# A channel-attention and gated-unit kernel: first chunk's weights kept on chip, squares of the second batch moved late, v's sums by DMA, first loads cut smaller

## The chip, the cores and the metric

The kernel runs on one core of a Trainium2 chip. The metric is the device time of one execution in microseconds (us), the median of three runs.

## The reference

For each of 4 batches, q, k and v are 6080 x 256 (tokens x channels). The columns of q and k are normalised over the tokens, their 256 x 256 product (over the tokens) goes through a softmax, and v is multiplied by it. The result, 24320 tokens of 256, goes through a gated unit with 2048 hidden columns:

```python
qn = q / (norm(q, axis=1) + 1e-6); kn = k / (norm(k, axis=1) + 1e-6)
a = softmax(kn.transpose(0, 2, 1) @ qn / tau)      # 256 x 256 a batch
x = (v @ a).reshape(24320, 256)
h = x @ w_in                                       # 256 -> 2048
out = (h * sigmoid(1.702 * h)) @ w_out             # 2048 -> 256
```

w_in and w_out come as 64-bit floats; the kernel reads their 32-bit words and makes float32 of them on chip.

## The kernel before, in words

The attention is folded into the weights: a batch's 256 x 256 softmax is multiplied into w_in once (`weights`, matmuls on line 744), and the tokens of v go straight through that product. Every float32 operand of these products is split in a high and a low part (`cast` on ScalarE, line 304, then `low` on VectorE, line 333), and a product is three matmuls (`three`, line 875): high-high, high-low, low-high. All the products of the main part are therefore on line 875.

A batch's 6080 tokens are worked in 6 chunks of up to 1024 columns, and a chunk in 8 pairs, each a pair of 128-column blocks of w_in. So there are 4 x 6 x 8 = 192 pairs, numbered by `place`. A pair has a front (seven products of v's parts and the weights, into the PSUM banks X, Y and Z, then the gate) and a back (the gated values times w_out, into banks O2, O3, O4, O7 and K). Front and back use a two-by-two scheme with seven products in place of eight, for which sums of v's quarters are made: `values` makes four of them a chunk on VectorE (lines 835, 836, 840 and 844) and splits seven operands. The very first chunk has a back with eight plain products (`FIRST`), so that the sums of w_out's blocks are not needed yet.

The scores of a batch: q and k come in tiles of 128 tokens. For batches 0 and 1 (`direct`) the tiles are multiplied as float32 (line 552) while ScalarE squares them and VectorE adds the squares to `acc` (line 312 by the helper); a unit is two tiles, there are 25 of them, and 4 tiles are one load into one of four staging buffers (gr0, gj0, gr1, gj1). Batch 0 does this at the very start, batch 1 right behind it and during the first chunk. Batches 2 and 3 do theirs in between the pairs of the batches ahead (`scores_at`), split in high and low parts (line 558), with the squares added to `acc` by accumulating DMAs from GpSimd's queue (`add_dma`, line 327), as are K's partial sums (`ka`, `kb`, `kc`). After the scores come the norms, the softmax (`finish`, in three steps) and the eight `weights`.

The weights' words: `win_convert` loads the words of a group of two pairs, for each half of the input rows; seven VectorE instructions make float32 and its low part, the result goes through the buffer "hl" to DRAM (`win_d`), and `weights` loads it from there. `wout_convert` does the same for one pair of w_out, with the sums of its blocks, through "hl" to `wout_d`; `fetch_wo` loads from there. The first group and the first two of w_out are converted at the start, the others during the first chunk.

The order of all work is set by a planner (`Plan`). Each piece of work is a node with an engine, a guessed cost, its predecessors and a due time; buffers are slots that a new user can have when the users of the old one are done. A list placement, repeated backwards and forwards, gives each node a start, and the program is issued in that order, each engine working through its own queue in order. Loads and stores are issued on the SP queue (line 292), accumulating DMAs on GpSimd's. So every edit to nodes moves the whole order.

Of the kernel before, what the change touches and what calls it, by code (L numbers as in the profile page):

```python
# [11 lines left out]
F32 = mybir.dt.float32  # L12
# [8 lines left out]
P = 128  # L21
# [19 lines left out]
class Node:  # L41
    __slots__ = ("eng", "cost", "lag", "fn", "deps", "uses", "due", "idx", "start", "left", "ready", "outs")

    def __init__(self, eng, cost, fn, deps, uses, due, lag, idx):
        self.eng, self.cost, self.fn, self.due, self.lag, self.idx = eng, cost, fn, due, lag, idx
        self.deps = [d for d in deps if d is not None]
        self.uses = list(uses)
        self.start = None


class Plan:
# [27 lines left out]
    def graph(self):  # L79
# [111 lines left out]

VSUM = lambda b, c: False
QSUM = lambda b: b >= 2
HIACT = True
TURNED = True
TAILX = True
STQ = False
# [20 lines left out]
def channel_attention_then_glu(  # L218
# [61 lines left out]
    win_d = dr.tile([NPAIR, P, 2, NC2, 2 * P], F32, name="win_d")  # L280
    wout_d = dr.tile([NPAIR, P, 2, NA + 1, P], F32, name="wout_d")
    w_d = [dr.tile([NPAIR, P, 2, NA - 1, P], F32, name=f"w_d{i}") for i in range(B)]
# [53 lines left out]

    g.add("DVE", 150, lambda: nc.vector.memset(ones, 1.0), due=-9e9)
    g.add("DVE", 60, lambda: nc.vector.memset(half, 0.5), due=-8e9)
    const_i = g.add("POOL", 2000, lambda: make_identity(nc, ident), due=-9e9)

    def full_bank(slot, due):

        b = bank(slot, "x")

        def fn():
            for i in range(HW // P):
                nc.tensor.matmul(
                    b()[:, i * P : (i + 1) * P], lhsT=ones, rhs=ones, start=i == 0, stop=True, skip_group_check=True,
                )

        return g.add("PE", 880, fn, (), [b], due)

    def keep_warm(n, deps, due, slot):
# [5 lines left out]

        return g.add("PE", 220 * n, fn, deps, [b], due)  # L360

# [62 lines left out]

    win_ready = {}

    def win_convert(grp, c, due, slot, lows, after=()):
# [9 lines left out]
        st = [  # L437
            load(
                lambda a=a: win_d[2 * grp + a, :, :, c, :],
                lambda a=a: hl()[:, :, a * 2 * P : (a + 1) * 2 * P], 256, [l], [hl], due + 1,  # L440
            )
# [6 lines left out]

    def wout_convert(u, due, slot, lows, after=()):
        raw = sbuf(slot, [P, 2, C, 2], U32, "words")  # L450
# [6 lines left out]
        n = to_float32(first, lows, raw, rs, due, True, f)  # L457
        st = sbuf("hl", [P, 2, 8, P], F32R, "cs")
        n = sums(f, [n], [f], due + 0.7)
        h = cast(lambda: st()[:, 0], lambda: f(), 8 * P, [n], [f, st], due + 1)  # L460
        l = low(lambda: st()[:, 1], lambda: f(), lambda: st()[:, 0], 8 * P, [h], [f, st], due + 1.1)
        wout_ready[u] = load(lambda: wout_d[u], lambda: st(), 1024, [l], [st], due + 1.2)


    class Attention:
# [19 lines left out]
        def load_direct(self, t0, room, slot, due):  # L485
            nt = min(room, T - t0)
            t = sbuf(slot, [P, 2, RT, C], F32, "raw4")
            cuts = range(nt + 1) if t0 == 0 else (0, nt)
            ns = []
            for a, z in zip(cuts, cuts[1:]):  # L490
                for i in range(2):
# [3 lines left out]
                    ))  # L495
            for o in range(nt):
                self.raw[t0 + o] = (t, o, ns[2 * o : 2 * o + 2] if len(ns) > 2 else ns)
            if nt < room and TAIL:
# [6 lines left out]
        def unit(self, u, due, after=()):  # L505
# [37 lines left out]
            for j in range(nt):  # L543
# [24 lines left out]
                news.append(n)  # L568
            if u == 0:
                self.acc_n = [g.add(  # L570
# [21 lines left out]
            else:  # L592
# [7 lines left out]
                    )  # L600
                ]

        def finish(self, slot):
# [128 lines left out]
    def weights(at, u, due, after=(), slot="Z", kept=None):  # L732

        wi = sbuf("wi", [P, 2, NC2, 2 * P], F32R, "wi")
        r = load(lambda: wi(), lambda: win_d[u], 512, [*win_ready[u], *after], [wi], due - 10)
        pb = bank(slot, "w")

        def fn():
            for i in range(NC2):
                ci = slice(i * P, (i + 1) * P)  # L740
                n = 0
                for l, m in ((0, 0), (0, 1), (1, 0)):
                    for j in range(NC2):
                        nc.tensor.matmul(  # L744
                            pb()[:, i * 2 * P : (i + 1) * 2 * P], lhsT=at.aT()[:, l, j, ci], rhs=wi()[:, m, j, :],
                            start=i == 0 and n == 0, stop=True, skip_group_check=True,
                        )
                        n += 1

        n = g.add("PE", 1440, fn, [at.a_h, at.a_l, r], [at.aT, wi, pb], due)  # L750
        f = sbuf(f"ra{u % 2}", [P, 8, P], F32, "wf")
# [368 lines left out]
    def fetch_wo(ck, p, u, due, after=()):  # L1120
        is_s = ck.kinds[p][2]
        cut = slice(1, 1 + NI) if is_s else slice(0, 4)

        def make(i):
            w = sbuf(f"wo{i}", [P, 2, NI, P], F32R, "wo")
            n = load(
                lambda: w()[:, :, : cut.stop - cut.start], lambda: wout_d[u, :, :, cut, :], 640,
                [wout_ready[u], *after], [w], due,
            )
            return w, n  # L1130

        return wo_slots.get((u, is_s), make)

    held = [None, {}]

    def fetch_wb(ck, p, pairs_of, due, after=()):
# [9 lines left out]
        if u not in places:  # L1146
            i = len(places)
            n = load(
                lambda: w()[:, i], lambda: wout_d[u, :, :, 1 + NI :, :], 256, [wout_ready[u], *after], [w], due,
            )  # L1150
# [33 lines left out]
    for u in range(2):  # L1184
        wout_convert(u, -55 + 4 * u, f"gi{u}", "oc1")
    nxt = Attention(1)
# [5 lines left out]
    for u in range(nu):  # L1192
        nxt.unit(u, -40 + 4.5 * u)


# [16 lines left out]
    def softmax_at(b, i):  # L1212
# [6 lines left out]
        return fn  # L1219

    def weights_at(b, u):
# [13 lines left out]
    for b in range(B):  # L1235
        for s in range(total):
# [56 lines left out]
```

## Time and profile before

| | |
|---|---|
| runs | 2083.36, 2083.2, 2081.8 us; median 2083.2 |
| the profiled execution's own time | 2082.57 us |
| its span, from first to last instruction | 2080.8 us |
| granted TensorE clock over the span | 0.999 |
| TensorE, VectorE, ScalarE, GpSimd busy | 99%, 95%, 83%, 5% |
| DMA | 457.76 MB, mean 220 GB/s |

A row of a view names the line, the engine (PE is TensorE, DVE VectorE, ACT ScalarE, POOL GpSimd, SPq the SP queue), the operation, the tile written and the tiles read, then its numbers. Busy time is the union of the instructions' drawn lengths; the ends of matmuls are modelled, since they overlap in the engine's pipeline.

### The profile page before, as it was taken

How to read it: one execution, taken by the hardware profiler on the slowest of the kernel's cores; microseconds unless marked ns; L12 is line 12 of the kernel's file. 1: busy time of each engine (PE TensorE's matmuls, PEld its weight loads, DVE VectorE, ACT ScalarE, POOL GpSimd, SP SyncE). 2: the span in 40 equal slices, each digit the busy share in tenths (PEclk: the TensorE clock that was granted, in tenths of full speed). 3: DMA queues.
4: the chain of work that ended last, by engine and by line, in shares of the span. 5: the costliest groups of instructions: out<-in, count | busy, mean ns of one | idle time of the engine just before them, and what ended most of it. 6: DMA issues, size and time to landing. Idle time of an engine off the chain costs nothing.

```text
span 2080.8 us, 27525 instructions
## 1 busy us (share of the span) xinstructions
PE 2055.2 (99%) x9556; PEld 1716.9 (83%) x9556; DVE 1970.5 (95%) x2457; ACT 1730.1 (83%) x2505; POOL 110.6 (5%) x127
## 2 busy tenths in 40 slices
PE   9899999999999999999999999999999999999999
PEld 8788888888888888888888888878888888888887
DVE  8997999999999999999999999999999999999898
ACT  6677888888888888888888888888888788888786
POOL 0000000010110100000000000010000000000000
PEclk9999999999999999999999999999999999999999
DMA  9986877778787666786777867648557555545545
GB/s 361 372 311 233 284 251 243 216 199 252 196 263 233 174 196 230 243 262 190 212 224 220 260 198 202 196 153 301 204 175 229 179 167 162 197 154 165 192 145 156
DMA packets 200314, 457.76 MB, mean 220 GB/s; under 512 B 17520, under 2 KB 87408, under 8 KB 199152
## 3 DMA queue, kind: packets, MB, share of 16 engines
q1 hardware_dynamic: 183072, 414.25, 57.2%
q0 software_dynamic: 17104, 41.75, 11.2%
q8 instruction: 76, 1.25, 0.2%
q14 instruction: 62, 0.51, 0.1%
HBM read 347.34 MB, written 66.85 MB: 199 GB/s over the span
## 4 chain that ended last, share of the span: by engine, by line
PE 74%; DVE 15%; ACT 4%; DMA 3%; issue 3%; SPq 0%; POOL 0%; DVEq 0%; ACTq 0%
PE ps_o L875 20%; PE ps_X L875 15%; PE ps_k L875 14%; PE ps_Z L875 10%; PE ps_Y L875 10%; DVE gp L312 3%; PE ps_s L558 3%; DVE gi L333 2%; DVE ga L312 2%; PE ps_w L744 2%; DVE acc L312 1%; DVE gr L333 1%; DVE gj L333 1%; DMA raw<-in_k 1%; ACT ga L902 1%
## 5 line engine op out<-in xcount | busy, mean ns | idle before, releaser
L875 PE MATMUL ps_X<-v,w 128*128 128x512 f32 (+1 forms) x1728 | 485.7, 389 | 2.1 <-ACT ps_Z L304 1.6
L875 PEld LDWEIGHTS ps_X<-v,w 128*128 128x128 f32 x1728 | 320.6, 188 | 70.3 <-ACT ps_Z L304 5.1
L333 DVE TENSOR_TENSOR gi<-ga,gi 128x1536 fp32r<-128x1536 f32 (+2 forms) x192 | 329.5, 1716 | 12.8 <-ACT gi L304 12.5
L902 ACT ACTIVATE ga<-ga 128x512 f32<-128x512 f32 (+1 forms) x384 | 238.7, 628 | 110.4 <-DVE ga L312 108.7
L875 PE MATMUL ps_Y<-v,w 128*128 128x512 f32 (+1 forms) x1152 | 324.7, 390 | 1.6 <-ACT ps_Y L304 1.6
L875 PE MATMUL ps_Z<-v,w 128*128 128x512 f32 (+1 forms) x1152 | 324.0, 389 | 1.0 <-ACT wf L304 0.5
L875 PE MATMUL ps_o<-gi,wo 128*128 128x512 f32 (+1 forms) x1200 | 322.4, 388 | 1.0 <-DVE oc L318 1.0
L875 PE MATMUL ps_o<-gj,wo 128*128 128x512 f32 (+1 forms) x1152 | 314.2, 388 | 1.5 <-DVE oc L312 1.0
L875 PE MATMUL ps_k<-gr,wb 128*128 128x512 f32 (+1 forms) x1104 | 293.2, 388 | 0.0
L304 ACT CAST gi<-ga 128x1536 fp32r<-128x1536 f32 (+2 forms) x192 | 279.1, 1454 | 4.7 <-PE ps_k L875 1.9
L875 PEld LDWEIGHTS ps_o<-gi,wo 128*128 128x128 f32 x1200 | 224.7, 188 | 47.1 <-DVE oc L318 1.8
L875 PEld LDWEIGHTS ps_Z<-v,w 128*128 128x128 f32 x1152 | 215.5, 188 | 46.3 <-ACT ps_Z L304 1.0
L875 PEld LDWEIGHTS ps_o<-gj,wo 128*128 128x128 f32 x1152 | 215.4, 188 | 45.1 <-DVE oc L312 1.4
L875 PEld LDWEIGHTS ps_Y<-v,w 128*128 128x128 f32 x1152 | 213.3, 188 | 47.5 <-ACT ps_Y L304 6.2
L875 PEld LDWEIGHTS ps_k<-gr,wb 128*128 128x128 f32 x1104 | 206.6, 188 | 41.0 <-DVE kb L312 0.2
L312 DVE TENSOR_TENSOR gp<-ga 128x1024 f32<-128x1024 f32 (+1 forms) x184 | 222.8, 1211 | 16.0 <-ACT ga L902 12.9
L333 DVE TENSOR_TENSOR gr<-gp,gr 128x1024 fp32r<-128x1024 f32 (+1 forms) x184 | 222.6, 1210 | 16.1 <-ACT gr L304 16.0
L333 DVE TENSOR_TENSOR gj<-gp,gj 128x1024 fp32r<-128x1024 f32 (+1 forms) x184 | 222.6, 1210 | 11.7 <-ACT gj L304 10.9
L304 ACT CAST gr<-gp 128x1024 fp32r<-128x1024 f32 (+1 forms) x184 | 191.5, 1041 | 30.1 <-DVE gp L312 27.5
L304 ACT CAST gj<-gp 128x1024 fp32r<-128x1024 f32 (+1 forms) x184 | 191.5, 1040 | 18.6 <-DVE gp L312 16.1
L875 PE MATMUL ps_k<-gi,wo 128*128 128x512 f32 (+1 forms) x552 | 155.0, 389 | 0.5 <-DMA wo<-wout_d 0.2
L304 ACT COPY ps_Y<-ps_X 128x512 f32<-128x512 f32 (+1 forms) x192 | 110.8, 577 | 31.3 <-PE ps_X L875 29.9
(127 smaller groups left out, 2721.6 us busy)
## 6 DMA issues: line engine op xcount, KB each, us to landing
w<-w_d SPq DMA_DIRECT2D x144, 768.0 KB, 5.0
wo<-wout_d SPq DMA_DIRECT2D x118, 640.0 KB, 5.2
wb<-wout_d SPq DMA_DIRECT2D x129, 256.0 KB, 4.1
acc<-raw POOLq DMA_DIRECT2D x44, 512.0 KB, 6.3
v_raw<-in_vT SPq DMA_DIRECT2D x20, 1024.0 KB, 7.7
out_T<-oc SPq DMA_DIRECT2D x80, 256.0 KB, 3.0
w<-w_d SPq DMA_DIRECT2D x144, 128.0 KB, 4.1
w_d<-wst SPq DMA_DIRECT2D x24, 768.0 KB, 5.2
```

The source lines that it names most:

```text
L304: return g.add("ACT", act(n, psum), lambda: nc.scalar.copy(dst(), src()), deps, uses, due)
L312: return g.add("DVE", dve(n), lambda: nc.vector.tensor_tensor(dst(), a(), b(), op=op), deps, uses, due)
L333: lambda: nc.vector.tensor_tensor(dst(), src(), hi().bitcast(F32), op=ALU.subtract),
L558: nc.tensor.matmul(out, lhsT=hl()[:pp, 1, j, l, ci], rhs=hl()[:pp, 0, j, r, :], start=begin and m == 0, stop=True, skip_group_check=True,)
L744: nc.tensor.matmul(pb()[:, i * 2 * P : (i + 1) * 2 * P], lhsT=at.aT()[:, l, j, ci], rhs=wi()[:, m, j, :], start=i == 0 and n == 0, stop=Tr ...
L875: nc.tensor.matmul(dst, lhsT=l(a), rhs=r(b), start=begin and n == 0, stop=True, skip_group_check=True,)
L902: lambda: nc.scalar.activation(dst(), src(), AF.Gelu_apprx_sigmoid, scale=sign), deps, uses, at,
```

## The change

1. Weights of the first chunk. `weights` of batch 0 reads the parts straight from "hl", which now holds a whole group (both halves) until both of its pairs have used it. `wout_convert` writes the first four blocks into the buffer that the first chunk's products read (`wo0` to `wo2`) and the sums into "wi"; both are still stored to DRAM for later chunks. It is called once a pair instead of twice every second pair.
2. Late squares. For units 12 to 24 of batch 1 the scores are made as before, without squares. Scores and squares so far are then copied out of their buffers (`turn`), and the missing squares are made during pairs 8 to 19 from a second load of q and k, added by accumulating DMA (`squares`). The softmax of batch 1 moves from pairs 7 to 9 to pairs 21 to 23, its weights from 10 to 17 to 24 to 31, and batch 2's scores from 19 to 59 to 31 to 59.
3. v's sums. For batches 1 to 3, `values` takes its other branch (lines 818 to 834): the four sums are made by accumulating DMAs, three of them through one buffer.
4. First loads. The first load of two tiles becomes one of four, cut in 1, 1 and 2 tiles; the order of the loads of the first eight tiles is fixed in the plan (`follows`); the first words of w_in wait until tiles 4 to 7 have landed, those of w_out until tiles 8 to 11 have. ScalarE loads its table for squares at the very start by a tiny instruction.

```diff
+            for d in n.follows:
+                ins[n.idx].append((d.idx, d.cost))
+                outs[d.idx].append((n.idx, d.cost))
...
-VSUM = lambda b, c: False
+VSUM = lambda b, c: b >= 1
 QSUM = lambda b: b >= 2
 HIACT = True
 TURNED = True
+NQ = 12
+SPANS = {1: (8, 20), 2: (31, 60), 3: (74, 118)}
...
+    g.add("ACT", 1400, lambda: nc.scalar.activation(rtau, half[:, :1], AF.Square), [half_n], (), -8e9)
...
-        hl = sbuf("hl", [P, 2, 4 * P], F32R, "cw")
-        h = cast(lambda: hl()[:, 0], lambda: wf(), 4 * P, [n], [wf, hl], due + 0.7)
-        l = low(lambda: hl()[:, 1], lambda: wf(), lambda: hl()[:, 0], 4 * P, [h], [wf, hl], due + 0.8)
+        if c == 0:
+            win_parts[grp] = (sbuf("hl", [P, NC2, 2, 4 * P], F32R, "cw"), [])
+        hl, done = win_parts[grp]
+        h = cast(lambda: hl()[:, c, 0], lambda: wf(), 4 * P, [n], [wf, hl], due + 0.7)
+        l = low(lambda: hl()[:, c, 1], lambda: wf(), lambda: hl()[:, c, 0], 4 * P, [h], [wf, hl], due + 0.8)
+        done.append(l)
...
-        st = sbuf("hl", [P, 2, 8, P], F32R, "cs")
+        wo = sbuf(f"wo{i}", [P, 2, NI, P], F32R, "wo")
+        st = sbuf("wi", [P, 2, 4, P], F32R, "cs")
+        h = cast(lambda: wo()[:, 0, :4], lambda: f()[:, :4], 4 * P, [n], [f, wo], due + 0.7)
+        l = low(lambda: wo()[:, 1, :4], lambda: f()[:, :4], lambda: wo()[:, 0, :4], 4 * P, [h], [f, wo], due + 0.8)
         n = sums(f, [n], [f], due + 0.7)
-        h = cast(lambda: st()[:, 0], lambda: f(), 8 * P, [n], [f, st], due + 1)
-        l = low(lambda: st()[:, 1], lambda: f(), lambda: st()[:, 0], 8 * P, [h], [f, st], due + 1.1)
-        wout_ready[u] = load(lambda: wout_d[u], lambda: st(), 1024, [l], [st], due + 1.2)
+        hs = cast(lambda: st()[:, 0], lambda: f()[:, 4:], 4 * P, [n], [f, st], due + 1)
+        ls = low(lambda: st()[:, 1], lambda: f()[:, 4:], lambda: st()[:, 0], 4 * P, [hs], [f, st], due + 1.1)
+        wout_ready[u] = (
+            load(lambda: wout_d[u, :, :, :3], lambda: wo()[:, :, 1:4], 384, [l], [wo], due + 1),
+            load(lambda: wout_d[u, :, :, 3:], lambda: st(), 512, [ls], [st], due + 1.2),
+        )
+        return wo, l
...
-            cuts = range(nt + 1) if t0 == 0 else (0, nt)
+            cuts = (0, 1, 2, nt) if t0 == 0 else (0, nt)
...
-            if u == 0:
+            if self.b == 1 and u >= NQ:
+                pass
+            elif u == 0:
...
+        def turn(self, due):
+
+            old, S = self.acc, self.S
+            acc = sbuf("acc", [P, 2, UT, C], F32, "acc")
+            total = sbuf("ss", [P, HW], F32, "ss")
+            self.acc_n = [cast(lambda: acc(), lambda: old(), 2 * UT * C, self.acc_n, [old, acc], due)]
+            self.last = [cast(lambda: total(), lambda: S(), HW, self.last, [S, total], due + 0.1, psum=True)]
+            self.acc, self.S = acc, total
+
+        def squares(self, u, due, after):
+
+            t0, nt, pp = self.units[u]
+            t = sbuf(f"ra{u % 2}", [P, 2, UT, C], F32, "raw")
+            acc = self.acc
+            view = lambda i: t()[:pp, i, :nt, :]
+            ns = [
+                load(
+                    lambda i=i: view(i) if pp == P else view(i)[:, 0], lambda i=i: self.rows(i, t0, nt, pp), 128 * nt,
+                    after, [t], due - 10, 7000,
+                )
+                for i in range(2)
+            ]
+            both = lambda: t()[:pp, :, :nt, :]
+            n = g.add(
+                "ACT", act(2 * nt * C), lambda: nc.scalar.activation(both(), both(), AF.Square), ns, [t], due,
+            )
+            self.acc_n = [add_dma(lambda: acc()[:pp, :, :nt, :], both, [n, *self.acc_n], [t, acc], due + 1)]
...
-        wi = sbuf("wi", [P, 2, NC2, 2 * P], F32R, "wi")
-        r = load(lambda: wi(), lambda: win_d[u], 512, [*win_ready[u], *after], [wi], due - 10)
+        if kept:
+            wi, r = win_parts[u // 2]
+            part = lambda m, j: wi()[:, j, m, u % 2 * 2 * P : (u % 2 + 1) * 2 * P]
+        else:
+            wi = sbuf("wi", [P, 2, NC2, 2 * P], F32R, "wi")
+            r = [load(lambda: wi(), lambda: win_d[u], 512, [*win_ready[u], *after], [wi], due - 10)]
+            part = lambda m, j: wi()[:, m, j, :]
...
+    def first_wo(u, *args):
+        wo_slots.get((u, False), lambda i: wout_convert(u, i, *args))
...
-    sizes = [UT] + [RT] * ((T + 1 - UT + RT - 1) // RT)
+    sizes = [RT] * ((T + 1 + RT - 1) // RT)
...
-            win_convert(0, 0, EARLY + t0 + 6, "ga0", "oc1")
+            win_convert(0, 0, EARLY + t0 + 6, "ga0", "oc1", at.raw[RT][2])
         if r == 6:
-            win_convert(0, 1, EARLY + t0 + 6, "ga1", "oc1")
+            win_convert(0, 1, EARLY + t0 + 6, "ga1", "oc1", at.raw[RT][2])
+    firsts = [n for o in (0, 1, 2, RT) for n in at.raw[o][2]]
+    for a, n in zip(firsts, firsts[1:]):
+        n.follows = [a]
...
-        wout_convert(u, -55 + 4 * u, f"gi{u}", "oc1")
+        first_wo(u, -55 + 4 * u, f"gi{u}", "oc1", at.raw[2 * RT][2])
...
+    if NQ < nu:
+        nxt.turn(-40 + 4.5 * nu)
...
-    for b, (begin, end) in {1: (0, 6), 2: (19, 60), 3: (74, 118)}.items():
-        if b >= 2:
-            for u in range(nu):
-                plan(begin + int(u * (end - begin) / nu), scores_at(b, u))
+    for b, (begin, end) in SPANS.items():
+        for u in range(NQ if b == 1 else 0, nu):
+            at_ = begin + int((u - NQ) * (end - begin) / (nu - NQ)) if b == 1 else begin + int(u * (end - begin) / nu)
+            plan(at_, squares_at(u) if b == 1 else scores_at(b, u))
...
-                for uu in (2 * grp, 2 * grp + 1):
-                    wout_convert(uu, t + 9 + 5 * (uu % 2), "vr", "oc1")
+            if b == c == 0 and u + 2 < NPAIR:
+                first_wo(u + 2, t + 9, "vr", "oc1")
```

## Rows read from the trace of the kernel before

**Rows 1.** The page, part 1: busy us (share of the span) xinstructions, by engine.

```profile
PE 2055.2 (99%) x9556; PEld 1716.9 (83%) x9556; DVE 1970.5 (95%) x2457; ACT 1730.1 (83%) x2505; POOL 110.6 (5%) x127
```

**Rows 2.** Timeline, TensorE, steady part: start us, us drawn, instruction.

```profile
1493.27 0.84 PE L875 MATMUL ps_Y<-v,w 128*128 128x512 f32 x3
1493.95 0.84 PE L875 MATMUL ps_X<-v,w 128*128 128x512 f32 x3
```

**Rows 3.** Stretches: length, each engine's busy us (x), PEclk, DMA share, GB/s.

```profile
0.00:50.00 50.00, 46.51 (x212) 40.45 (x213) 40.45 (x55) 30.87 (x33) 0.70 (x6) 1.00 0.97 359
50.00:90.00 40.00, 31.71 (x167) 27.28 (x165) 39.48 (x79) 25.93 (x37) 2.09 (x1) 0.96 1.01 374
90.00:320.00 230.00, 228.11 (x1088) 189.58 (x1088) 213.80 (x327) 185.34 (x279) 3.81 (x4) 1.00 0.79 278
320.00:800.00 480.00, 478.39 (x2268) 402.00 (x2268) 463.26 (x553) 417.63 (x601) 39.11 (x43) 1.00 0.71 212
800.00:2060.00 1260.00, 1254.46 (x5757) 1044.40 (x5756) 1197.41 (x1427) 1063.63 (x1549) 64.07 (x72) 1.00 0.64 204
2060.00:2080.80 20.80, 16.01 (x73) 13.23 (x71) 16.14 (x21) 6.70 (x9) 0.86 (x1) 1.00 0.43 129
```

**Rows 4.** TensorE's waits, 0 to 130 us: us in total, times, longest us.

```profile
PE ps_s L552 <- DMA raw<-in_k: 9.2, 6, 4.4
...
PE ps_x L358 <- DVE half L338: 1.1, 1, 1.1
```

**Rows 5.** The chain of waits, 45 to 100 us: start us, us, what.

```profile
78.39 6.53 DMA raw<-in_k
...
85.05 5.14 PE ps_s L552 x16
```

**Rows 6.** Timeline of the SP queue's issues at the start.

```profile
3.08 0.43 SPq L292 DMA_DIRECT2D words<-in_w_in  x1
3.55 0.43 SPq L292 DMA_DIRECT2D raw<-in_k  x1
```

**Rows 7.** Timeline of TensorE at the start, with the idle time before it.

```profile
10.07 35.18 PE L552 MATMUL ps_s<-raw 128*128 128x256 f32 x160 [1.96 <-DMA raw<-in_k]
```

**Rows 8.** VectorE groups, 51.6 to 89 us: xcount, busy us, mean ns, idle.

```profile
L312 DVE TENSOR_TENSOR acc<-acc,raw 128x1024 f32<-128x1024 f32 x8 | 9.8, 1221 | 0.0
...
L333 DVE TENSOR_TENSOR cs<-cf,cs 128x1024 fp32r<-128x1024 f32 x2 | 2.4, 1214 | 0.0
```

**Rows 9.** VectorE groups of the whole run, by shape; same columns.

```profile
L312 DVE TENSOR_TENSOR v_raw<-v_raw 128x512 f32<-128x512 f32 x40 | 27.5, 688 | 0.2
L312 DVE TENSOR_TENSOR acc<-acc,raw 128x1024 f32<-128x1024 f32 x22 | 26.9, 1223 | 0.0
...
L312 DVE TENSOR_TENSOR acc<-acc,raw 128x512 f32<-128x512 f32 x1 | 0.7, 683 | 0.0
```

**Rows 10.** DMA issues: xcount, KB each, median us to landing.

```profile
acc<-raw POOLq DMA_DIRECT2D x44, 512.0 KB, 6.3
...
raw<-in_q SPq DMA_DIRECT2D x46, 256.0 KB, 5.3
```

**Rows 11.** Instructions on v_raw: xcount: ns min/median/max, first and last start.

```profile
L292 SPq DMA_DIRECT2D v_raw<-in_vT x24: 383/386/1125, 41.8 to 1933.4; - x24
```

**Rows 12.** TensorE's waits, 800 to 2060 us.

```profile
PE ps_Y L875 <- ACT ps_Y L304: 1.4, 2, 1.0
...
PE ps_o L875 <- DVE oc L312: 1.0, 1, 1.0
```

**Rows 13.** Instructions on ka, K's first partial sum, and its DMAs' landing.

```profile
L327 POOL DMA_DIRECT2D ka<-oc x23: 847/862/1052, 257.8 to 2048.3; - x23
...
DMA to landing us min/median/max: 3.2/4.5/8.7
```

**Rows 14.** Waits of GpSimd's queue: us in total, times, longest us.

```profile
POOL ka L327 <- ACT oc L304: 546.1, 17, 82.7
POOL acc L327 <- ACT raw L581: 430.7, 35, 26.5
```

More of the change, by code (lines that the diff above doesn't have):

```diff
@@ L41 @@
 class Node:
-    __slots__ = ("eng", "cost", "lag", "fn", "deps", "uses", "due", "idx", "start", "left", "ready", "outs")
+    __slots__ = ("eng", "cost", "lag", "fn", "deps", "uses", "due", "idx", "start", "follows")
     def __init__(self, eng, cost, fn, deps, uses, due, lag, idx):
@@ L48, in __init__ @@
         self.start = None
+        self.follows = ()
 class Plan:
@@ L280, in channel_attention_then_glu @@
     win_d = dr.tile([NPAIR, P, 2, NC2, 2 * P], F32, name="win_d")
-    wout_d = dr.tile([NPAIR, P, 2, NA + 1, P], F32, name="wout_d")
+    wout_d = dr.tile([NPAIR, P, 2, NA, P], F32, name="wout_d")
     w_d = [dr.tile([NPAIR, P, 2, NA - 1, P], F32, name=f"w_d{i}") for i in range(B)]
@@ L335, in low @@
         )
-    g.add("DVE", 150, lambda: nc.vector.memset(ones, 1.0), due=-9e9)
-    g.add("DVE", 60, lambda: nc.vector.memset(half, 0.5), due=-8e9)
+    ones_n = g.add("DVE", 150, lambda: nc.vector.memset(ones, 1.0), due=-9e9)
+    half_n = g.add("DVE", 60, lambda: nc.vector.memset(half, 0.5), due=-8e9)
+    g.add("ACT", 1400, lambda: nc.scalar.activation(rtau, half[:, :1], AF.Square), [half_n], (), -8e9)
     const_i = g.add("POOL", 2000, lambda: make_identity(nc, ident), due=-9e9)
@@ L349, in fn @@
                 )
-        return g.add("PE", 880, fn, (), [b], due)
+        return g.add("PE", 880, fn, [ones_n], [b], due)
     def keep_warm(n, deps, due, slot):
@@ L358, in fn @@
                 nc.tensor.matmul(b()[:, :P], lhsT=ones, rhs=ones, start=True, stop=True)
-        return g.add("PE", 220 * n, fn, deps, [b], due)
+        return g.add("PE", 220 * n, fn, [*deps, ones_n], [b], due)
     def to_float32(out, lows, raw, ready, due, flat, outbuf):
@@ L425, in channel_attention_then_glu @@
     win_ready = {}
+    win_parts = {}
     def win_convert(grp, c, due, slot, lows, after=()):
@@ L439, in win_convert @@
                 lambda a=a: win_d[2 * grp + a, :, :, c, :],
-                lambda a=a: hl()[:, :, a * 2 * P : (a + 1) * 2 * P], 256, [l], [hl], due + 1,
+                lambda a=a: hl()[:, c, :, a * 2 * P : (a + 1) * 2 * P], 256, [l], [hl], due + 1,
             )
@@ L447, in channel_attention_then_glu, with wout_convert @@
     wout_ready = {}
-    def wout_convert(u, due, slot, lows, after=()):
+    def wout_convert(u, i, due, slot, lows, after=()):
         raw = sbuf(slot, [P, 2, C, 2], U32, "words")
@@ L495, in load_direct @@
                     ))
-            for o in range(nt):
-                self.raw[t0 + o] = (t, o, ns[2 * o : 2 * o + 2] if len(ns) > 2 else ns)
+            for j, (a, z) in enumerate(zip(cuts, cuts[1:])):
+                for o in range(a, z):
+                    self.raw[t0 + o] = (t, o, ns[2 * j : 2 * j + 2])
             if nt < room and TAIL:
@@ L744, in fn @@
                         nc.tensor.matmul(
-                            pb()[:, i * 2 * P : (i + 1) * 2 * P], lhsT=at.aT()[:, l, j, ci], rhs=wi()[:, m, j, :],
+                            pb()[:, i * 2 * P : (i + 1) * 2 * P], lhsT=at.aT()[:, l, j, ci], rhs=part(m, j),
                             start=i == 0 and n == 0, stop=True, skip_group_check=True,
@@ L748, in fn @@
                         n += 1
-        n = g.add("PE", 1440, fn, [at.a_h, at.a_l, r], [at.aT, wi, pb], due)
+        n = g.add("PE", 1440, fn, [at.a_h, at.a_l, *r], [at.aT, wi, pb], due)
         f = sbuf(f"ra{u % 2}", [P, 8, P], F32, "wf")
@@ L1120, in fetch_wo @@
     def fetch_wo(ck, p, u, due, after=()):
-        is_s = ck.kinds[p][2]
-        cut = slice(1, 1 + NI) if is_s else slice(0, 4)
         def make(i):
+            assert ck.kinds[p][2]
             w = sbuf(f"wo{i}", [P, 2, NI, P], F32R, "wo")
[L1126 to L1129, printed above, removed]
+            n = load(lambda: w(), lambda: wout_d[u, :, :, :NI, :], 640, [*wout_ready[u], *after], [w], due)
             return w, n
-        return wo_slots.get((u, is_s), make)
+        return wo_slots.get((u, ck.kinds[p][2]), make)
+    def first_wo(u, *args):
+        wo_slots.get((u, False), lambda i: wout_convert(u, i, *args))
     held = [None, {}]
@@ L1148, in fetch_wb @@
             n = load(
-                lambda: w()[:, i], lambda: wout_d[u, :, :, 1 + NI :, :], 256, [wout_ready[u], *after], [w], due,
+                lambda: w()[:, i], lambda: wout_d[u, :, :, NI:, :], 256, [wout_ready[u][1], *after], [w], due,
             )
```

2 lines of the change are left out of this document (added).

## The prediction, made before the changed kernel was run

> **What bounds the kernel now.** I read the busy shares first. TensorE is busy 2055.2 of 2080.8 us, VectorE 1970.5, ScalarE 1730.1 [rows 1]. So TensorE is full and VectorE nearly so, and the first question is whether TensorE's 99% is work. In the steady part its groups of three matmuls start 0.68 us apart, stretch after stretch, while each group is drawn 0.84 us long [rows 2]. A matmul therefore starts every 0.227 us, no gap is left there, and the drawn end hides up to 0.16 us of any stop. The change takes no matmul out and adds none to the products, so it can only give back time in which TensorE stands still: 25.6 us by its busy time (2080.8 - 2055.2), plus about 0.16 us for every stop.
>
> Next I read where these 25.6 us lie, from the table of stretches [rows 3]. The idle time of TensorE (length minus busy) is 3.5 us in 0 to 50, 8.3 in 50 to 90, 1.9 in 90 to 320, 1.6 in 320 to 800, 5.5 in 800 to 2060, and 4.8 in the last 20.8, most of it the tail after the last matmul. In the 40 us from 50 to 90, 2% of the run, lies a third of it. What ends it there comes third: in the list of waits of the first 130 us TensorE waits 9.2 us for rows of k (six times, 4.4 at the longest) [rows 4]. The chain of waits shows why the longest one is late: the load of k is issued at 78.39, lands after 6.53 us, and TensorE starts at 85.05 [rows 5]; by the code its staging buffer comes free with an addition of squares on VectorE. VectorE is busy 39.48 of those 40 us [rows 3]. So from 50 to 90 VectorE's queue is the bound, through the buffers that its additions free. This stretch is also the only one whose granted clock is below 1.00, 0.96 as a mean [rows 3]: some of it ran at 1.2 instead of 2.4 GHz.
>
> **Smaller first loads, in order, words behind.** Today the queue issues 512 KB of words at 3.08, and only then the k rows of the second load at 3.55 [rows 6]; TensorE then stops for 1.96 us before 10.07 [rows 7]. After the change tiles 2 and 3 come as two loads of 256 KB, and no words start until tiles 4 to 7 have landed. The new wait sits on the SP queue, where loads behind the words could be held; the planner places the words by it, and tiles behind them have four buffers. Bounds: 0 (DMA is at a share of 0.97 of these 50 us [rows 3], so the bytes may only trade places) to -2.4 (all idle but the 1.1 us that TensorE waits for its constant [rows 4]). I take -2.0, nearest to the stop seen. The early loading of ScalarE's table lies before the first data and costs nothing; if the first data came sooner, it would be in the way for its own length.
>
> **First chunk's weights on chip.** The eight loads of wo, 512 KB each, go, and so do the first batch's eight loads of wi (512 KB): 8 MB less in a stretch where DMA stands at 1.0 [rows 3]. The low half of w_out's words is cut in two: one instruction of 1.21 us [rows 8] becomes two of about 0.69 [rows 9], +0.16 us on VectorE eight times, 1.3 us in all, and ScalarE pays about as much. The price is coupling: the words of a w_in group now stay in "hl" until both of its pairs have been multiplied, so the next group's conversion ends after that. Its chain is seven VectorE instructions of 512 columns, at most 0.69 us each [rows 9], 4.8 us, with queued work between them. Where TensorE still has scores of the second batch to do, that is covered; uncovered once, it costs 5 us. The same block has a good side: conversions that VectorE does between 50 and 90 today, ahead of need, have no buffer to go to and fall behind the first weights.
>
> **Late squares.** Units 12 to 24 of the second batch lose their addition on VectorE: 11 full ones at 1.223 us and two short ones at 0.68 [rows 9], 14.8 us, about half of VectorE's squares work for that batch. Of the 90-us opening only units below 12 have had their additions (eight of them, 9.8 us [rows 8]), so the relief comes after 90; before 90 it acts only through the order, since VectorE no longer has to run ahead. Added: 13 reloads of q and k, 13 squares on ScalarE, 13 accumulating transfers of 512 KB landing in 6.3 us [rows 10], and two copies on ScalarE. They lie in pairs 8 to 19, some 200 to 320 us, where DMA has room (mean 0.79 from 90 to 320 [rows 3]).
>
> For 50 to 90 together I take -5.0: half of the 8.3 us, 4.1, with six stops at 0.16. Bounds: -9 (all stops) to +5 (one uncovered conversion). For 90 to 320 I take -1.0 of 1.9; bounds -1.9 to +2.
>
> The scores of the third batch are squeezed from pairs 19 to 59 into 31 to 59: 25 units over 29 pairs instead of 41, 0.86 a pair instead of 0.61. Per pair that is 0.25 more units, each with one instruction of 1024 columns and one of 512 on VectorE, 1.22 + 0.69 us [rows 9], 0.48 us, in a stretch where VectorE is busy 463.3 of 480 us [rows 3], 96.5%. A pair lasts some 10.3 us (the loads of v, one a chunk of eight pairs, come 1891.6/23 = 82.2 us apart [rows 11]), and TensorE's share of a pair grows as well, so VectorE goes to about 98%, not over. I take +1.0 for 320 to 800; bounds -1 to +4.
>
> **v's sums by DMA.** In the 18 chunks of batches 1 to 3 four sums of 0.69 us leave VectorE: 72 of them, 49 us. Each chunk gets one load and four accumulating transfers of 256 KB instead. From 800 to 2060 VectorE is busy 1197.4 of 1260 us [rows 3], 95%, and would fall to about 91%. TensorE's 5.5 us of idle there are short waits on ScalarE and VectorE, 1.0 us at the longest [rows 12]; I take -2.5, bounds -5.5 to the price of the last rival below. The added bytes (1.28 MB a chunk) meet a DMA share of 0.64 and are hidden; they show if that share nears 1 at the chunk borders.
>
> **Sum.** -2.0 - 5.0 - 1.0 + 1.0 - 2.5 = -9.5 us. The span becomes 2071.3. The profiled execution took 2082.57 us, 1.77 more than its span, so 2073.1 by its own time; the median of the runs is 0.6 above that execution, so 2083.2 - 9.5 = 2073.7 us.
>
> **Rivals.**
> Late stops go as well: with VectorE at 91% nearly all visible idle time returns, at every term's lower bound: -2.4 - 9 - 1.9 - 1 - 5.5 = -19.8, 2063.4 us. For it: these stops sit on ScalarE and VectorE. Against: ScalarE gets no relief from v's sums, and the longest entry among TensorE's late waits names it [rows 12].
>
> The opening keeps its bound: VectorE stays full from 50 to 90, the same additions of units below 12 still free the same buffers, and the first loads' gain is waited away there. Then only +1.0 and -2.5 are left: 2081.7 us, no change that can be told. For it: nothing that VectorE must do before 90 is taken out. Against: what it does ahead of need loses its place.
>
> The accumulating sums come late: slower. Three of the four go one after the other through one buffer (v_t), each waiting on GpSimd's queue, for its landing, and for a split: 0.86 issue + 4.5 landing [rows 13] + 1.3 for cast and low, three times 6.7 = 20 us, behind a load of 5.3 us [rows 10], so 25 us; at the longest landing, 8.7, it is 38. The lead is from the third pair to the end of the eighth, 5 pairs of 10.3 us = 52. It decides when GpSimd's queue holds one of them for more than some 14 to 27 us; that queue has waited in total 430.7 us for squares (35 times) and 546.1 for copies of K (17 times, 82.7 at the longest) [rows 14], and what stands behind such a wait is held with it. The price is a first product that waits at each of 18 borders; at 1.0 us each, the longest single wait that TensorE has there [rows 12], 18 us: -7 + 18 = +11, 2094 us. Against: the waits of that queue are mostly for work that is not due.
>
> The Trainium skill, "DMA: Bandwidth & Descriptors", section "Anatomy of one DMA — SWDGE (gpsimd) path", gives a transfer issued from GpSimd a fixed 2.0 us and its bytes over 436 GB/s; an estimate of 2.6 us for 256 KB. By it the serial part would be 3 x 4.8 = 14 us, and this last rival would want 38 us of holding. The trace disagrees: 3.2 us is the least and 4.5 the median [rows 13], so the trace's price stands above.
>
> **How the numbers follow.** Forecast 0.46, with its own range 2068 to 2079; late stops as well 0.13; opening keeps its bound 0.24; sums late 0.17. A measurement of this kernel tells about 0.2%, 4.2 us, from no change: faster is below 2079.0, slower above 2087.4. Faster is forecast and first rival, 0.59; same 0.24; slower 0.17. The range 2062 to 2088 leaves out most of the last case and the end of the first rival's, under 2 in 10.
>
> **What would show it.** First loads right: no stop before 10 us, the first batch's last score 2 us earlier. Opening right: idle time of TensorE from 50 to 90 near 4 us and the first product of the chunk well before 90; wrong: VectorE still full there and a k load behind an addition. Coupling wrong: a stop before the third or fifth pair's weights that a word's low half ends. Sums right: VectorE near 91% after 800 and no TensorE stop that a v tile ends; wrong: such stops every eighth pair, with GpSimd's transfer as the releaser. The forecast falls if TensorE's idle time is spread otherwise than these stretches have it, or if the new order of the whole plan, which every edit moves, opens stops where none was.

## The result: slower, 2094.96 us

The changed kernel took 2094.96 us (median of 5 runs, 2091.77 to 2097.05), the kernel before 2081.80 beside it (2080.54 to 2083.36): a ratio of 1.0059, 95% interval [1.0045, 1.0074]. The forecast was 2073.7, in a range of 2062 to 2088. The profiled run took 2095.48 us, its span is 2093.7.

The page after, part 1, as in [rows 1]:

```profile
PE 2064.9 (99%) x9556; PEld 1719.1 (82%) x9556; DVE 1926.0 (92%) x2380; ACT 1734.2 (83%) x2518; POOL 183.1 (9%) x212
```

VectorE lost 44 us of work, as meant, and the kernel lost 13 us of time. The table of stretches after, to be laid beside [rows 3]:

```profile
0.00:50.00 50.00, 47.06 (x212) 41.13 (x212) 36.88 (x46) 30.35 (x33) 0.70 (x6) 0.97 0.93 325
50.00:90.00 40.00, 39.95 (x217) 34.91 (x217) 38.26 (x77) 28.07 (x44) 1.42 (x1) 1.00 0.92 330
90.00:320.00 230.00, 228.75 (x1041) 188.71 (x1040) 213.68 (x311) 191.94 (x292) 15.91 (x17) 1.00 0.87 275
320.00:800.00 480.00, 471.89 (x2258) 393.47 (x2257) 451.80 (x562) 411.02 (x594) 48.81 (x56) 1.00 0.79 234
800.00:2060.00 1260.00, 1248.54 (x5706) 1036.88 (x5705) 1159.12 (x1357) 1054.50 (x1531) 113.68 (x130) 1.00 0.74 218
```

Idle time of TensorE from 50 to 90 is 0.05 us (8.3 before), but from 320 to 800 it is 8.1 (1.6), and from 800 to 2060 11.5 (5.5). DMA's share rose in both of the late stretches, 0.71 to 0.79 and 0.64 to 0.74.

Drawn idle time is not enough here: summed over the span it grew by 3.2 us only (28.8 against 25.6), the span by 12.9. Drawn ends hide part of each stop, and matmuls at half clock are drawn as busy. So I added up from the traces, for every matmul, the distance from its start to the next one's, less the usual distance of its form (0.227 us for 512 columns). The usual distances sum to 2035.3 us in both kernels (within 0.2 us in all the kernels for which the sum is quoted here); what is above them is stops, and they carry the difference: 52.4 - 39.7 = 12.7 us. All tables of stops below are worked out in this way.

| stops of TensorE, us | 0 to 320 | 320 to 800 | 800 to end | sum |
|---|---|---|---|---|
| before | 21.5 | 4.2 | 14.0 | 39.7 |
| after | 9.5 | 16.5 | 26.5 | 52.4 |

The opening gives 12 us, more than forecast. Each of the two later stretches takes 12 us back. Who ends those stops, in the list of TensorE's waits after, 320 to 2060 us:

```profile
PE ps_o L931 <- DVE oc L319: 3.5, 2, 3.3
PE ps_t L748 <- ACT ga L958: 3.2, 1, 3.2
PE ps_Z L931 <- ACT wf L311: 2.9, 2, 2.8
PE ps_Y L931 <- DVE ga L319: 2.1, 2, 1.6
```

No v tile and no GpSimd transfer stands in that list: the forecast's slow case is not what happened, and that its time, 2094, came out is chance. The chain of waits tells why ScalarE and VectorE were late, here at 825 and at 994 us:

```profile
813.83 10.61 DMA w_d<-wst
...
824.54 0.94 ACT wst L823
825.48 0.94 ACT gj L311
826.42 0.95 ACT gr L311
827.37 0.49 ACT wf L311
...
827.91 1.65 PE ps_Z L931 x3
...
982.30 10.74 DMA out_T<-oc
...
993.07 0.70 DVE oc L319
...
993.81 4.61 PE ps_o L931 x12
```

A store of new weights (w_d<-wst) lands after 10.61 us. ScalarE's next cast needs its buffer; two casts of pairs under way and a copy of the next weights stand behind that cast in ScalarE's queue, and TensorE needs the last of them. At 982 it is a store of outputs, and VectorE waits. The median landing of out_T<-oc stores of 256 KB rose from 3.0 to 4.5 us, that of acc's transfers from 6.3 [rows 10] to 7.2. From 320 to 2060 ScalarE's waits for a wst store grew from 0.3 to 9.5 us and VectorE's for an out_T store from 1.8 to 8.2. Their lists there, first before, then after (us in total, times, longest us):

```profile
ACT wst L767 <- DMA w_d<-wst: 0.3, 1, 0.3
...
DVE oc L312 <- DMA out_T<-oc: 1.8, 1, 1.8
```

```profile
ACT wst L823 <- DMA w_d<-wst: 9.5, 4, 3.8
...
DVE oc L319 <- DMA out_T<-oc: 8.2, 6, 4.4
```

The median landing of the wst stores hardly moved in that stretch (6.0 to 6.1 us, both sizes together); their longest went from 8.0 to 10.8 us, that of the out_T stores from 8.6 to 12.4. From the list of DMA issues (count, KB each, median us to landing) first four rows of after, then one of before:

```profile
acc<-raw POOLq DMA_DIRECT2D x55, 512.0 KB, 7.2
...
out_T<-oc SPq DMA_DIRECT2D x80, 256.0 KB, 4.5
...
v_t<-in_vT POOLq DMA_DIRECT2D x45, 256.0 KB, 5.7
...
v_raw<-in_vT POOLq DMA_DIRECT2D x15, 256.0 KB, 8.1
```

```profile
out_T<-oc SPq DMA_DIRECT2D x80, 256.0 KB, 3.0
```

### The profile page after: what moved, and what is told of

It reads as the page before. It is cut to its first block, busy times and chain, and to the rows that moved or that the text cites. A ratio compares the mean times of both kernels' runs of the same rounds, so it can differ in the third digit from the quotient of the medians.

```text
span 2093.7 us, 27783 instructions
## 1 busy us (share of the span) xinstructions
PE 2064.9 (99%) x9556; PEld 1719.1 (82%) x9556; DVE 1926.0 (92%) x2380; ACT 1734.2 (83%) x2518; POOL 183.1 (9%) x212
## 3 DMA queue, kind: packets, MB, share of 16 engines
q8 instruction: 76, 1.25, 0.2%
## 4 chain that ended last, share of the span: by engine, by line
PE 78%; DVE 9%; ACT 6%; DMA 4%; issue 2%; SPq 0%; DVEq 0%; ACTq 0%
PE ps_o L931 19%; PE ps_X L931 15%; PE ps_k L931 15%; PE ps_Z L931 10%; PE ps_Y L931 10%; PE ps_s L573 4%; PE ps_s L579 3%; DVE gp L319 2%; DVE gi L340 2%; DMA w_d<-wst 2%; PE ps_w L800 2%; ACT ga L958 1%; DVE ga L319 1%; DMA raw<-in_k 1%; DMA out_T<-oc 1%
## 5 line engine op out<-in xcount | busy, mean ns | idle before, releaser
L311 ACT CAST gj<-gp 128x1024 fp32r<-128x1024 f32 (+1 forms) x184 | 191.5, 1041 | 15.6 <-DVE gp L319 15.2
```

Of the source, the lines that this page charges most:

```text
L311: return g.add("ACT", act(n, psum), lambda: nc.scalar.copy(dst(), src()), deps, uses, due)
```

## The experiments

Theories: A, v's sums load DMA, so stores land late and ScalarE or VectorE stand at the heads of their queues; B, the third batch's scores, squeezed behind the second batch's last weights, stall TensorE (B': through "hl", which the first scores share with the last wst stores); C, each issue order has its own accidents. Ratios are to the kernel before, run beside each, with 95% intervals.

**Parts taken out.** e1_no_vsum:

```diff
-VSUM = lambda b, c: b >= 1
+VSUM = lambda b, c: False
```

> The changed kernel with v's sums back on VectorE in all chunks; the rest of the change stays. Theory A (v's accumulating transfers crowd the DMA, so stores of weights and outputs land late and ScalarE and VectorE wait at the head of their queues): the 12.5 us of extra TensorE stops after 800 us go, 2082 us; the stores of wst land in about 5 us again (6.1 in the changed kernel). Theory B (the squeeze of the third batch's scores into pairs 31 to 59, behind the late squares, costs it): no more than 2 us back, 2093. Theory C (any edit gives another order with its own accidents): anything from 2075 to 2095, with stops that no transfer ends.

e2_no_late (all squares of the second batch at the start, scores where they were):

```diff
-NQ = 12
-SPANS = {1: (8, 20), 2: (31, 60), 3: (74, 118)}
+NQ = 25
+SPANS = {1: (0, 6), 2: (19, 60), 3: (74, 118)}
```

> The changed kernel without the late squares: all 25 units of the second batch squared and added at once, batch 1's softmax and batch 2's scores at their old pairs; v's sums stay on DMA. Theory A: the stops after 800 us stay, those of 320 to 800 fall; with some of the opening's gain of 10 us lost, 2085 to 2092. Theory B: the 12 us of extra stops between 320 and 800 go and most of the rest, 2080 to 2083. Theory C: anything.

e3_no_both is both edits.

> The changed kernel with neither: first chunk's weights on chip and the first loads alone. Theories A and B together: stops after 320 us as in the kernel before (18 us), and the opening's gain kept in part (5 to 10 us): 2072 to 2077. If the opening's gain hangs on the late squares: 2082.

e4_before_vsum adds the sums alone to the kernel before:

```diff
-VSUM = lambda b, c: False
+VSUM = lambda b, c: b >= 1
```

> The kernel before with v's sums by DMA in batches 1 to 3, and nothing else. Theory A: 8 to 13 us slower, 2090 to 2095, with stores of wst and outputs that land later. Theory B: no change or a gain of up to 3 us, since VectorE gets 49 us back: 2079 to 2082.

Measured: e1 2079.24 us, 0.9982 [0.9973, 0.9991]; e2 2078.70, 0.9979 [0.9970, 0.9988]; e3 2075.43, 0.9964 [0.9952, 0.9977]; e4 2085.08, 1.0011 [1.0002, 1.0020]. Without both parts the change is faster. One alone costs 3 to 4 us, both together 20: more than the sum, which called for other orders. e3 is where A and B together put it. e1 is 3 us below what A gave, e2 below what A and B gave, and e4 costs 3.0 us where A gave 8 to 13: A has the sign, but not the size. The wst stores, said there to land in about 5 us "again", had a median of 6.0 us before the change too.

**Same work, other orders.** e5_turns8 repeats the planner's search 8 times in place of 4:

```diff
-    TURNS = 4
+    TURNS = 8
```

> The changed kernel, same work, the planner given 8 rounds of placing in place of 4, so that it issues everything in another order. Theory A+B (the edits themselves cost it: crowded DMA together with squeezed scores): 2090 to 2098 again, with stops of TensorE near those places. Theory C (an accident of this one order): away from 2095 by more than 5 us, most likely 2078 to 2088.

e6_hop60:

```diff
-    HOP = 70
+    HOP = 60
```

> The changed kernel, same work, another order: the planner's cost for a step from one engine to another is 60 ns in place of 70. As with 8 rounds: A+B 2090 to 2098; C away from 2095 by more than 5 us, and not the same as with 8 rounds.

e12_neither_turns8 is e3 with TURNS = 8, m1_sums_turns8 is e2 with it, m2_late_turns8 e1, m4_before_turns8 the kernel before.

> The run with neither late squares nor v's sums (2075.4), same work in another order: 8 rounds of placing in place of 4. Theory C at the size of the two re-ordered runs of the changed kernel (4 and 8 us away): 2071 to 2083. If an order changes less where nothing is tight: within 2 us of 2075.

> The changed kernel with the squares of the second batch made at the start, as before (v's sums by DMA stay), in the other issue order (the planner's search repeated 8 times in place of 4). Theory 'interaction' (the sums crowd DMA, and that hurts only where late squares and squeezed scores also want it): about 2079, within 4 us of the 2078.7 of the first order, and 800 to the end with 14 to 18 us of stops. Theory 'lucky order' (v's sums by themselves cost 8 or more and the first order hid it): 2086 or more, with stops behind stores from 800 on as in the changed kernel.

> The changed kernel with v's sums on VectorE, late squares kept, in the other issue order. 'Interaction': about 2079, within 4 us, stops of 8 to 12 us between 320 and 800. 'Lucky order': 2086 or more, with 14 us or more of stops between 320 and 800.

> The kernel before in the other issue order, no work changed. If order alone moves a few us: 2079 to 2087, and TensorE busy 30 to 34 of the 40 us from 50 to 90, as in the first order. If the opening's stops were an accident of the order: 2076 or less, with 37 us or more there.

Measured: e5 2087.18 us, 1.0030 [1.0019, 1.0041]; e6 2091.32, 1.0042 [1.0027, 1.0057]; e12 2078.95, 0.9982 [0.9972, 0.9991]; m1 2087.66, 1.0024 [1.0014, 1.0034]; m2 2079.15, 0.9984 [0.9975, 0.9992]; m4 2081.17, 0.9992 [0.9984, 1.0001].

e5 came out as C said, e6 as A and B together. e12 and m4 lie where order alone puts them. m1, with 27.0 us of stops after 800, fits 'lucky order'; m2, with 12.0 us from 320 to 800, fits 'interaction'.

| us, orders of 4 / 8 turns | v's sums on VectorE | by DMA |
|---|---|---|
| squares early | 2075.4 / 2079.0 | 2078.7 / 2087.7 |
| squares late | 2079.2 / 2079.2 | 2095.0 / 2087.2 |

In the second order the two parts add up (0.2 and 8.7 alone, 8.2 together): the interaction of the first order is not there, so it doesn't belong to the parts as such. Which of the two orders was the lucky one can't be told from two. The sums cost 3.3, 15.7, 8.7 and 8.0 us in the table, 3.0 in e4 and 6.2 between e10 and e9 below: one sign in all six pairs. Late squares cost 3.8, 16.3, 0.2 and -0.5; they cost nothing in the second order because their stops and gains cancel there. The stops by stretch show it. A trace is of one execution; those of e1 and e5 were the fastest of their kernels, 4.5 and 2.5 us under the medians.

| stops, us | 0 to 320 | 320 to 800 | 800 to end |
|---|---|---|---|
| before, m4 | 21.5, 21.9 | 4.2, 2.7 | 14.0, 12.7 |
| neither: e3, e12 | 15.8, 20.6 | 3.9, 3.5 | 13.9, 11.7 |
| late: e1, m2 | 10.4, 11.6 | 10.9, 12.0 | 10.5, 12.6 |
| sums: e2, m1 | 14.0, 14.3 | 5.5, 5.5 | 16.9, 27.0 |
| both: after, e5, e6 | 9.5, 6.8, 13.6 | 16.5, 14.0, 19.7 | 26.5, 21.0, 16.4 |
| before and sums: e4 | 21.8 | 5.5 | 14.8 |
| both, border or lag changed: e7, e9, e8 | 16.9, 15.6, 12.5 | 10.2, 6.0, 30.0 | 15.5, 17.9, 26.1 |
| late, border moved: e10 | 12.6 | 6.2 | 14.7 |
| first chunk's weights alone: e11, m3 | 14.6, 16.8 | 2.8, 2.9 | 12.1, 12.9 |

With late squares and the change's border (third batch's scores from pair 31) the middle stretch has 10 to 30 us of stops, without late squares 3 to 5.5, in every order. With v's sums the last stretch has 15 to 27 us, without them 10.5 to 14.7; e4, at 14.8, is hardly apart from the kernels without. In m1, another order with early squares, stores of the same two kinds open stops at the same two places, 818 and 990 us, as its chain of waits shows:

```profile
807.75 9.47 DMA w_d<-wst
...
817.32 0.94 ACT wst L823
818.26 0.49 ACT ps_Y L311
...
818.80 1.04 PE ps_Y L931 x3
...
981.62 8.80 DMA out_T<-oc
...
990.44 0.70 DVE oc L319
...
991.19 1.22 PE ps_o L931 x2
```

The stores show in nearly every order. From 320 to 2060 the median landing of the out_T stores is 4.5 to 5.3 us in eight of the nine kernels with the sums by DMA (3.8 in e8), and 2.6 to 3.7 in the nine without. From 800 to 2060 ScalarE and VectorE wait for stores of the two kinds 6.8 to 17.2 us in those eight, and 1.6 to 3.3 in the nine without. e8 is the exception: it has no such wait after 800 and 26.1 us of stops all the same, most of them behind copies and splits of ScalarE and VectorE.

So A is shown as a cost from 800 on; how hard it hits, and what else stops TensorE there, is C. Whether the added bytes or the adding itself makes the stores late, no run separates.

**The border of weights and scores.** e7_spread gives the third batch's scores more pairs, e9_gap also starts them three pairs later:

```diff
-SPANS = {1: (8, 20), 2: (31, 60), 3: (74, 118)}
+SPANS = {1: (8, 20), 2: (31, 72), 3: (86, 130)}
```

> The changed kernel with the scores of the third batch spread over pairs 31 to 71 and of the fourth over 86 to 129, about as thin as in the kernel before, v's sums on DMA and late squares as they are. Theory B (the squeeze): the 12 us of extra stops between 320 and 800 go, and the rest falls too, 2078 to 2083. Theory A alone: 2088 to 2093, since the transfers of v's sums are all there. Theory C: anywhere.

```diff
-SPANS = {1: (8, 20), 2: (31, 60), 3: (74, 118)}
+SPANS = {1: (8, 20), 2: (34, 72), 3: (86, 130)}
```

> The changed kernel with three pairs between the second batch's last weights and the third batch's first scores (which go over pairs 34 to 71, the fourth's over 86 to 129); v's sums on DMA, late squares as they are. It differs from the spread run (31 to 71, 2085.7 us) in the gap. Theory B' (the scores' first parts wait in buffer hl for the last weights' store): the extra 6 to 10 us of stops between 320 and 800 go, 2078 to 2081, and no load, cast or store ends a stop at the first scores. Theory A (the sums' transfers): 2084 to 2088, little better than the spread run. Theory C: anywhere within 6 us of 2086.

e10_gap_no_vsum is e9 with v's sums on VectorE.

> As the gap run, with v's sums on VectorE. Theory B': opening as in the changed kernel (9.5 us of stops to 320, against 16 without late squares), 320 to 800 as in the kernel before (4 us), the rest 12: 2067 to 2072, the best so far. Theory C: no better than 2075, the run with neither late squares nor sums.

e8_lag9 tells the planner that each store of new weights or outputs holds its buffer for longer:

```diff
-            return load(dst, src, kb, deps, uses, due)
+            return load(dst, src, kb, deps, uses, due, 9000)
```

> The changed kernel with the planner told that stores of weights and outputs need 9 us to land in place of 4 (the trace has 6.1 and 4.5 in the median, 10.8 and 12.4 at the longest). Theory A (late landings hold ScalarE and VectorE at the head of their queues): the waits on w_d and out_T, 17.7 us in the changed kernel, fall under 6 and the time to 2080 to 2086. Theory B: 2090 or more, the squeeze is unchanged. Theory C: anywhere, whatever those waits do.

Measured: e7 2085.66 us, 1.0010 [0.9999, 1.0021]; e9 2081.84, 0.9994 [0.9984, 1.0003]; e10 2075.69, 0.9963 [0.9948, 0.9978]; e8 2109.71, 1.0132 [1.0117, 1.0147]. Stops from 320 to 800: 10.2 in e7, 6.0 in e9, 6.2 in e10, 30.0 in e8, against 16.5. Of those 16.5 us, 6.7 lie between 400 and 480 us, around pair 31, and 5.0 between 760 and 800, at the stop of 773 us told of further down, which is no part of the border. Between 400 and 480 us e7 has 5.6, e9 0.8 and e10 0.3 (the kernel before 1.1). So the gap removes the stops of the border; spreading the scores does not, and most of what e7 gains in this stretch is the stop at 773. e10 stayed 4 us above the range of B': 12.6 us of stops in the opening where 9.5 were expected, and 14.7 from 800 on where 12 were.

e8, meant to help, made B' plain. It missed what A gave for it: the waits for stores came to 12.7 us instead of under 6, all of them before 800, and the time to 2109.7. Its list of TensorE's waits and its chain at the border:

```profile
PE ps_s L579 <- ACT hl L311: 11.2, 1, 11.2
```

```profile
444.92 3.83 DMA w_d<-wst
...
448.85 0.95 ACT wst L823
449.82 1.10 DVE wst L340
...
451.51 3.84 DMA w_d<-wst
...
455.45 1.05 ACT hl L311
456.53 1.24 DVE hl L340
...
457.81 2.29 PE ps_s L579 x9
```

The last weights' stores hold "hl", the first scores' split waits for it, and TensorE's queue waits with it. In the changed kernel itself the chain of waits at that place runs through a load of q (7.29 us from 428.90) and the splits into "hl", not through a wst store. At this border a split of ScalarE into "hl" waits for a wst store in five kernels with late squares and scores from pair 31 (1.3 us in e1, 2.0 in e5, 4.4 in e6, 5.1 in e7, 5.7 in e8), and in none of the other thirteen. A long wait of TensorE on it is shown in e8 alone. That the border costs the changed kernel some 6 us (6.7 against 0.8) is shown by e9; through which wait stays open there. Giving the stores and the scores buffers of their own was not tried.

**The first chunk's weights alone.** e11_on_chip_only is e3 without the first loads:

```diff
-    g.add("ACT", 1400, lambda: nc.scalar.activation(rtau, half[:, :1], AF.Square), [half_n], (), -8e9)
...
-            cuts = (0, 1, 2, nt) if t0 == 0 else (0, nt)
+            cuts = range(nt + 1) if t0 == 0 else (0, nt)
...
-    sizes = [RT] * ((T + 1 + RT - 1) // RT)
+    sizes = [UT] + [RT] * ((T + 1 - UT + RT - 1) // RT)
...
-            win_convert(0, 0, EARLY + t0 + 6, "ga0", "oc1", at.raw[RT][2])
+            win_convert(0, 0, EARLY + t0 + 6, "ga0", "oc1")
```

and likewise the other waits and the fixed order. m3_on_chip_turns8 is e11 with TURNS = 8.

> The kernel before with the first chunk's weights on chip alone: without late squares, v's sums and the first loads. If the first loads give nothing (the stop at 8.7 us is still 2 to 3 us long with them): 2074 to 2077, as the run with both. If they give the forecast 2 us: 2077 to 2079. If the opening's gain is theirs (words out of the way of the rows): 2081.

> The kernel before with the first chunk's weights on chip and nothing else, in the other issue order. If the gain is the mechanism (fewer bytes and conversions between 50 and 90): 2070 to 2077, and 38 us or more of TensorE work in 50 to 90. If the 2072.35 was a lucky order: 2079 or more.

Measured: e11 2072.35 us, 0.9947 [0.9932, 0.9962]; m3 2074.92, 0.9961 [0.9949, 0.9973]. Both beat both kernels, in either order; e11 is the fastest of all, 10.5 us below the kernel before, and m3 is 7.1 below it (6.3 below m4, the same order). e11 and m3 are 3 and 4 us below e3 and e12, with intervals that overlap: the first loads give nothing and may cost. The stretch 50 to 90 of e11, and its VectorE additions of squares there:

```profile
50.00:90.00 40.00, 38.97 (x212) 34.35 (x212) 38.78 (x76) 30.09 (x45) 2.63 (x1) 1.00 0.89 306
```

```profile
L319 DVE TENSOR_TENSOR acc<-acc,raw 128x1024 f32<-128x1024 f32 x12 | 14.7, 1227 | 0.0
```

TensorE is idle 1.0 us instead of 8.3, with VectorE as full as before (38.78 of 40). What VectorE does has changed: 12 additions of squares in place of 8 [rows 8], so 4 more units free their buffers. m3 has the same 12 additions and 39.17 us of TensorE there, as its expectation said; the kernel before in the other order, m4, has 7 additions and 33.48 us (31.71 in [rows 3]), so order alone does not do this. Fewer bytes (306 GB/s there, 374 before) came together with fewer conversions; no run separates the two.

## Why the prediction was wrong, step by step

**Sums (-2.5 forecast; +12.5 us of stops from 800 on).** This step failed. VectorE fell to 92% of that stretch (1159.12 of 1260), close to the forecast's 91%, which put all 49 us into it; 38 lie there. No chunk's first product waited for a sum. But free VectorE time was worth nothing: in none of the six pairs did the sums gain time. What had a price was the sentence "the added bytes meet a DMA share of 0.64 and are hidden". The mean hid the peaks. From 804 to 828 us the share after is 1.01 and more:

```profile
804.00:816.00 12.00, 12.00 (x60) 10.14 (x59) 12.00 (x19) 10.67 (x17) 1.67 (x2) 1.00 1.01 318
816.00:828.00 12.00, 9.23 (x47) 7.54 (x46) 9.37 (x13) 6.74 (x10) 0.91 (x2) 0.97 1.05 367
```

Before, 800 to 830 already stands at 0.92 with 0.45 us of idle; that row should have been asked for. A high share alone doesn't tell which store is late, though: from 982 to 994, where the out_T store took 10.74 us, it is 0.91. The step looked for late readers of the sums, while the losers were stores of others, whose buffers an engine in strict order waits for. An accumulating transfer into v_raw lands after a median of 8.1 us, where the forecast took 4.5 from ka [rows 13]. The Trainium skill, "DMA: Bandwidth & Descriptors", section "Anatomy of one DMA — SWDGE (gpsimd) path", gives 2.0 us and the bytes over 436 GB/s, an estimate of 2.6 us for 256 KB; 5.7 and 8.1 us here disagree further than before. The case "accumulating sums come late" had the right sign and part, and the wrong place: its wait of v at 18 borders appears nowhere, though GpSimd's queue did wait for v_t (167.0 us in 27 waits on VectorE's splits).

**Late squares (+1.0 forecast from 320 to 800; +12.3 measured, about 7 of it without the sums).** This term was too small as well. It counted VectorE's added work per pair, and VectorE, forecast at about 98% of this stretch, was busy 94% of it (451.80 of 480). What it left out is that pair 31 carries the second batch's last weights and the third's first scores, which share "hl": 6.7 us of stops lie there. With the border moved by three pairs and more pairs for the scores they fall to 0.8, and the stretch to 6. Another 5.0 us come from one stop at 772.9 us and the low clock behind it, which no other order repeats at that size: ScalarE put gelus (the gate's function) between the softmax's exponentials and loaded its tables again, 1.28 us each. ScalarE's timeline after:

```profile
769.09 1.28 ACT L958 ACT_TABLE_LOAD   x1
770.38 0.60 ACT L958 ACTIVATE ga<-ps_Y 128x512 f32<-128x512 f32 x1
771.00 1.28 ACT L716 ACT_TABLE_LOAD   x1
...
774.27 1.28 ACT L958 ACT_TABLE_LOAD   x1
```

**50 to 90 (-5.0 forecast; idle 8.3 to 0.05, and 1.9 to 1.25 from 90 to 320).** Right in mechanism and too small: conversions done ahead of need fell back behind additions, the stated good side. Less right is the sentence that 8 MB go from a stretch where DMA stands at 1.0: of the sixteen loads that are gone, four were issued before 90 us, the others up to 190, where the share was 0.79. The coupling through "hl" cost nothing there, and VectorE, still full (38.26 of 40), did more of the additions that free buffers (10 in place of 8), so the rival 'opening keeps its bound' fell. Late squares do help the opening too (0 to 320: 10 to 12 us of stops in e1 and m2, 16 to 21 in e3 and e12), which the forecast put at 1.0 after 90; they lose it again behind 320.

**First loads (-2.0 forecast; no gain, and e11 and m3 are 3 to 4 us faster without them).** The term was worth nothing. The words are indeed issued late, but the stop only moved. The SP queue's issue and TensorE's first stop after, against [rows 6, 7]:

```profile
10.17 0.44 SPq L299 DMA_DIRECT2D words<-in_w_in  x1
```

```profile
11.10 5.16 PE L573 MATMUL ps_s<-raw 128*128 128x256 f32 x15 [1.88 <-DMA raw<-in_k]
```

The bound of 0, bytes that trade places at a DMA share of 0.97, was nearer than the -2.0 taken.

**What stays open.** Which stores will land late in a given order can't be read from the parts: the same work in two orders differs by 0 to 9 us. Why the squares cost 16 us in the first order with the sums and nothing in the second is not settled beyond the stops listed.

## What to carry to other kernels

Where the bound engine is full, work taken from a second engine is worth what the bound engine waits for it, and work given to DMA costs what it does to the landing of other transfers: look at the DMA share in windows of some 10 us and at the longest landings of stores, and ask for each store which engine's queue head waits for its buffer. Price an edit to a planned order in at least two orders of the same work, and with stops by stretch rather than by its total. Of a change of four parts, run each alone: here the first chunk's weights alone gave 7 to 10 us, and in the order that was built the other three parts together gave that back and 13 more.

## What the runs showed of the hardware that was not expected

A stop of TensorE can cost more than its length. Behind the stops at 11, 773, 825, 990 and 1438 us the granted clock is 0.50, 1.2 GHz in place of 2.4, for 3.4 us each, of which about half is lost. Windows and TensorE's timeline after, at 994 us:

```profile
994.60:998.00 3.40, 3.40 (x10) 2.64 (x9) 3.40 (x4) 1.06 (x1) 0.59 (x1) 0.51 1.00 247
```

```profile
993.81 0.97 PE L931 MATMUL ps_o<-gj,wo 128*128 128x512 f32 x3 [3.27 <-DVE oc L319]
994.61 1.45 PE L931 MATMUL ps_o<-gi,wo 128*128 128x512 f32 x3
995.85 2.57 PE L931 MATMUL ps_o<-gj,wo 128*128 128x512 f32 x6
998.26 0.84 PE L931 MATMUL ps_X<-v,w 128*128 128x512 f32 x3
```

TensorE counts as busy 3.40 of 3.40 us there. The nine matmuls from 994.61 take until the next start at 998.26, 3.65 us, where nine at 0.227 us take 2.04: 1.6 us are lost. The stops drawn before such stretches are 1.6 to 3.3 us long; the 1.96 us stop of the kernel before [rows 7] had none behind it, so these runs give no length from which it happens.
